# A convolution and a mixture of experts on one core: the outputs of the large tiles transposed by VectorE, stored in pieces, loaded back and gated on ACT

## The chip, the cores and the metric

The kernel runs on one core of one Trainium2 chip. Engines are named as in the profile: PE (TensorE), PEld (its weight loads), DVE (VectorE), ACT (ScalarE), POOL (GpSimd), SP (SyncE, which here only issues transfers). The metric is the device time of one execution in microseconds (us), median of several runs; smaller is better.

## The reference

```python
Xf = np.fft.rfft(x, n=2 * S, axis=1)            # x: 8 x 5696 x 128
y = np.fft.irfft(Xf * np.fft.rfft(h, n=2 * S, axis=0)[None], n=2 * S, axis=1)[:, :S]
x = y.reshape(B * S, D)                         # 45568 tokens of 128
logits = x @ w_gate + modality_bias[modality_id]
e_idx = np.argmax(logits, axis=1)
gate_w = softmax(logits)[np.arange(N), e_idx]
out[mask] = gate_w[mask, None] * (np.maximum(x[mask] @ w1[e], 0.0) @ w2[e])   # mask: tokens of expert e
```

A long convolution by Fourier transforms is followed by a layer of 8 experts (128 to 1024 to 128 features), where each token goes to one expert and its result is scaled by one gate value.

## The kernel before, in words

The program has two parts that overlap. The first (`stage1`, `stage23`, `stage4`) computes the convolution as two rounds of matrix products. Its last transform, `stage4`, makes token rows, finds each row's expert, position and gate value, and `dispatch` scatters the rows with indirect transfers from POOL into the DRAM array `rows`, where the tokens of one expert lie together. A row has 130 numbers: 128 features, the gate value, and the token's index in the output.

The second part (`Moe`) takes `rows` in tiles of consecutive tokens of one expert: 81 large tiles of 512 tokens (0 to 80 here) and then small ones of 256 tokens (81 to 100, and three more under a condition at run time). Tiles 0 to 35 belong to the first two levels, which are begun while `stage4` still produces rows; their outputs are held back (`NHELD`), stored to the DRAM array `late`, loaded again by `bring` into `ob`, and scattered later, between the outputs of later tiles.

A large tile t is worked in 8 steps (t, f), f = 0 to 7, a small one in 4. In a step PE runs `gemm1` (three products of 512 columns into a PSUM buffer `ph`: high and low parts of the float32 factors) and then `gemm2` of the step two earlier (three products into `po`, which gathers over all steps of a tile). From `ph`, ACT makes `hh` (relu, L647) and DVE makes `hl` (the low part, L648). So six products make a step, and `gemm2` of (t, 0) comes behind `gemm1` of (t, 2). `ph` has two PSUM buffers, and `po` has two. Once a tile, `prep` makes the operands of the next one: DVE transposes 32x32 blocks (`mxt`, L626; the 128-byte pieces in which the rows were loaded finish the transposition), ACT copies the high part (`mxh`, L629), DVE makes the low part (`mxl`, L630).

When a tile's `po` is done, ACT copies it to `ot` (L669), PE transposes it in four 128x128 pieces (`pxt`, L677), DVE multiplies by the gate value (`of`, L680), and POOL scatters 128 rows at a time to `out` (L709). For held tiles POOL also copies the indices into `held` (L683).

Order: within an engine, instructions run in program order. The SP queue is written out by hand: for each tile the weights of tile t+2 (2 MB, L613, taken only where the expert changes), the rows of tile t+3 (four transfers of 64 KB, L603, and one of gate values and indices, L605), then stores and loads of `late`. The order of ACT, DVE and POOL is set by a scheduler when the kernel is built; PE's too while `stage4` runs, and by hand behind it (tile 32 on in the program). `evenly` paces the scatters, a little under one a step, behind that step's ACT instruction.

Of the kernel before, what the change touches and what calls it, by code (L numbers as in the profile page):

```python
# [60 lines left out]
NLAST = 3  # L61
NHELD = LEVELS[0] + LEVELS[1]
SMALL = LEVELS[3] - NLAST
EVEN = ((NHELD + LEVELS[2]) * NSUB + SMALL * TSL // 128) / (8 * (LEVELS[2] - 2) + 4 * (SMALL - 3))
JOBS = [(lv, j) for lv, n in enumerate(LEVELS) for j in range(n)]
# [26 lines left out]
def conv_moe(  # L92
# [485 lines left out]
    class Moe:  # L578
        def __init__(self, wp, sp0, sp, pst, psh, pso):
            self.sp0, self.sp, self.pst, self.psh, self.pso = sp0, sp, pst, psh, pso  # L580
            self.slots = [wp[i].tile([128, 2, 2, FF], F32R, name=f"slot{i}") for i in range(NSLOT)]
            self.st = {}
# [3 lines left out]
            self.back, self.backs, self.credit = 0, [], 0.0  # L586

# [3 lines left out]
        def load(self, t):  # L591
            lv, j = JOBS[t]
            tab, src = self.tabs[lv]
            ts = TSL if lv == len(LEVELS) - 1 else TS
            ns = ts // 128
            r0 = nc.sync.value_load(tab[0:1, j:j + 1], min_val=0, max_val=E * REGION)
            rt = self.sp0.tile([128, TS], F32, name="mrt", bufs=4)
            mt = self.sp0.tile([128, NSUB, 2], F32, name="mmt", bufs=5)
# [6 lines left out]
            nc.sync.dma_start(mt[:, :ns], src[bass.ds(r0, ts), D:].rearrange("(c p) w -> p c w", p=128))  # L605
            self.st[t] = {"rt": rt, "mt": mt, "ts": ts, "ns": ns}
# [26 lines left out]
        def gemm1(self, t, f):  # L633
# [17 lines left out]
        def gemm2(self, t, f):  # L651
# [15 lines left out]
            if k == 7:  # L667
                ot = self.sp.tile([128, TS], F32, name="ot")
                nc.scalar.copy(ot[:, :ts], po)  # L669
                st["ot"] = ot  # L670

        def finish(self, t):
            st = self.st.pop(t)
            ns = st["ns"]
            pq = self.pst.tile([128, NSUB, 128], F32, name="pxt")
            for c in range(ns):
                nc.tensor.transpose(pq[:, c, :], st["ot"][:, c * 128:(c + 1) * 128], ident)  # L677
            of = self.sp.tile([128, NSUB, D], F32, name="of")
            rt = st["mt"]
            nc.vector.tensor_tensor(of[:, :ns], pq[:, :ns], rt[:, :ns, 0:1].to_broadcast([128, ns, D]), op=ALU.mult)  # L680
            ri = rt.bitcast(I32)
            if t < NHELD:
                nc.gpsimd.tensor_copy(self.held[:, t, :].unsqueeze(2), ri[:, :, 1:])  # L683
                nc.sync.dma_start(late_d[t], of.rearrange("p c d -> p (c d)"))
                return
            for c in range(ns):
                self.outs.append((t, c, ri[:, c, 1:2], of))

        def bring(self):
            if self.back < NHELD and len(self.backs) <= NSUB // 2:  # L690
                t = self.back
                self.back += 1
                of = self.sp.tile([128, NSUB, D], F32, name="ob")
                nc.sync.dma_start(of.rearrange("p c d -> p (c d)"), late_d[t])
                for c in range(NSUB):
                    self.backs.append((t, c, self.held[:, t, c:c + 1], of))

# [26 lines left out]
        def tiles(self, first, total):  # L724
# [11 lines left out]
            for g in range(len(steps) + LAG):  # L736
# [5 lines left out]
                if t < total:  # L742
                    self.gemm1(t, f)
                    dispatch(1, self.st[t]["act"])
                    self.evenly(self.st[t]["act"])
                    if t > NHELD:
                        self.bring()
                else:
                    self.scatter(1)
# [13 lines left out]
            if f < LAG:  # L763
                self.finish(total - 1)
            while self.outs or self.backs or self.back < NHELD:
                self.scatter(len(self.outs))
                self.outs, self.backs = self.backs, []
                self.bring()

# [10 lines left out]
    with tc.tile_pool(name="p4l", bufs=1, space=PSUM) as ps4l:  # L780
# [19 lines left out]
        with tc.tile_pool(name="moe", bufs=2) as sp, tc.tile_pool(name="moew", bufs=1) as wp, \  # L800
# [119 lines left out]
```

## Time and profile before

| | before |
|---|---|
| median of 3 runs | 2048.96 us (2048.7 to 2052.32) |
| the profiled execution | 2071.95 us; its span 2070.1 us |
| PE busy | 1976.8 us (95%) |
| DVE, ACT, POOL busy | 1448.5, 1129.2, 1115.2 us |
| mean granted TensorE clock | 0.984 |

Times in the views are counted from the start of the profiled span. A row of the timeline has start, duration, engine, line, operation and tiles, and in brackets the idle time before it with what ended it. A matmul's duration is longer than the distance to the next one's start, since they are pipelined. The profiled execution took 1% longer than the median run.

### The profile page before, as it was taken

To read this page: it belongs to the slowest core of one execution; us is meant where nothing else is said; L and a number is where in the kernel's file an instruction comes from. 1 tells how busy PE (TensorE), PEld (TensorE's weight loads), DVE (VectorE), ACT (ScalarE), POOL (GpSimd) and SP (SyncE) were. 2 spreads that over 40 slices of the span, in tenths; PEclk is the share of its full clock that TensorE was granted. 3 is DMA by queue.
4 is the path that set the end of the run, shared out by engine and by line. 5 is a ranking of instruction groups with operands and counts; after the bars stand their busy time and mean duration, and the time that the engine had idled before them with its cause. 6 is when DMAs were issued, how large, how long until landed. Compare 5 with 4: busy or idle time off the path is not lost. (4 is left out here: it accounts for less than half of the span.)

```text
span 2070.1 us, 32691 instructions
## 1 busy us (share of the span) xinstructions
PE 1976.8 (95%) x9114; PEld 1414.6 (68%) x9114; DVE 1448.5 (70%) x2478; ACT 1129.2 (55%) x2000; POOL 1115.2 (54%) x1085
## 2 busy tenths in 40 slices
PE   6889999999999997999999999999999999999996
PEld 5755555534444434878878778777787778778996
DVE  6659888886877996687677676756666666565553
ACT  5757777544444444666666566444544455454443
POOL 2127777673787783544344544614555555555544
PEclk9999999999999998999999999999999999999998
DMA  9999999989999997544465643353333343335443
GB/s 330 391 359 302 324 324 329 290 248 319 330 326 309 315 323 247 169 127 130 112 170 172 173 126 75 86 174 80 74 79 76 73 119 72 83 70 150 141 146 122
DMA packets 395831, 407.09 MB, mean 197 GB/s; under 512 B 242583, under 2 KB 277368, under 8 KB 393344
## 3 DMA queue, kind: packets, MB, share of 16 engines
q1 hardware_dynamic: 324496, 271.97, 44.3%
q10 hardware_dynamic: 47920, 85.94, 13.0%
q0 software_dynamic: 23232, 47.08, 6.6%
q8 instruction: 74, 1.21, 0.3%
q14 instruction: 109, 0.89, 0.1%
HBM read 396.70 MB, written 182.99 MB: 280 GB/s over the span
## 5 line engine op out<-in xcount | busy, mean ns | idle before, releaser
L648 DVE SCALAR_TENSOR_TENSOR hl<-ph,hh 128x512 fp32r<-128x512 f32 x728 | 496.1, 686 | 337.8 <-ACT hh L647 243.8
L647 ACT ACTIVATE hh<-ph 128x512 fp32r<-128x512 f32 x728 | 431.8, 598 | 469.2 <-PE ph L644 324.2
L320 POOL DMA_INDIRECT rows<-rt,idx x360 | 369.6, 1027 | 280.4 <-ACT hh L647 174.6
L290 POOL TENSOR_TENSOR t<-t,t 96x512 f32<-96x512 f32 x224 | 330.2, 1495 | 137.7 <-DVE t L283 120.1
L283 DVE TENSOR_TENSOR t<-px,hs 96x512 f32<-96x512 f32 x512 | 318.1, 677 | 63.1 <-PE px L280 27.2
L709 POOL DMA_INDIRECT out<-of,mmt x220 | 217.2, 987 | 222.2 <-ACT hh L647 172.6
L642 PE MATMUL ph<-mxh,slot 128*128 128x512 f32 (+1 forms) x808 | 319.9, 396 | 14.1 <-DVE hl L648 10.5
L664 PE MATMUL po<-hh,slot 128*128 128x512 f32 (+1 forms) x808 | 304.7, 377 | 8.3 <-ACT hh L647 8.2
L666 PE MATMUL po<-hl,slot 128*128 128x512 f32 (+1 forms) x808 | 300.7, 372 | 0.2 <-DVE hl L648 0.2
L644 PE MATMUL ph<-mxl,slot 128*128 128x512 f32 (+1 forms) x808 | 300.0, 371 | 0.0
L665 PE MATMUL po<-hh,slot 128*128 128x512 f32 (+1 forms) x808 | 299.6, 371 | 0.0
L643 PE MATMUL ph<-mxh,slot 128*128 128x512 f32 (+1 forms) x808 | 299.4, 371 | 0.0
L280 PE MATMUL px<-z,m 96*96 96x512 f32 x512 | 257.2, 604 | 4.0 <-DVE t L283 3.2
L263 ACT COPY ut<-pu 90x512 f32<-90x512 f32 x256 | 148.0, 581 | 127.5 <-PE pu L258 60.7
L709 POOL DMA_INDIRECT out<-ob,held x144 | 139.9, 971 | 121.5 <-ACT hh L647 81.8
L258 PE MATMUL pu<-t,mi 96*96 96x512 f32 x384 | 197.5, 606 | 4.7 <-ACT ut L263 2.1
L642 PEld LDWEIGHTS ph<-mxh,slot 128*128 128x128 f32 x808 | 152.6, 189 | 58.0 <-DVE hl L648 27.5
L664 PEld LDWEIGHTS po<-hh,slot 128*128 128x128 f32 x808 | 152.5, 189 | 38.2 <-ACT hh L647 12.1
L666 PEld LDWEIGHTS po<-hl,slot 128*128 128x128 f32 x808 | 152.4, 189 | 28.2 <-DVE hl L648 0.6
L644 PEld LDWEIGHTS ph<-mxl,slot 128*128 128x128 f32 x808 | 152.2, 188 | 28.0
L665 PEld LDWEIGHTS po<-hh,slot 128*128 128x128 f32 x808 | 152.6, 189 | 25.3
L643 PEld LDWEIGHTS ph<-mxh,slot 128*128 128x128 f32 x808 | 153.3, 190 | 18.0
(165 smaller groups left out, 2796.9 us busy)
## 6 DMA issues: line engine op xcount, KB each, us to landing
slot<-w12s SPq DMA_DIRECT2D x101, 2048.0 KB
z<-z SPq DMA_DIRECT2D x128, 360.0 KB
z<-z SPq DMA_DIRECT2D x45, 640.0 KB
z<-z SPq DMA_DIRECT2D x45, 512.0 KB
mrt<-rows SPq DMA_DIRECT2D x312, 64.0 KB
w12s<-ws ACTq DMA_DIRECT2D x32, 512.0 KB
u<-ua ACTq DMA_DIRECT2D x63, 256.0 KB
u<-ub ACTq DMA_DIRECT2D x63, 256.0 KB
```

The costliest lines, as they stand in the source:

```text
L283: prods[0] = nc.vector.tensor_tensor(prod[i, j].rearrange("p (b d) -> p b d", d=D), px[:KP].rearrange("p (b d) -> p b d", d=D), hs[:, j, k ...
L290: add = eng.tensor_tensor(y[:, i], y[:, i], prod[1, 1 - i], op=ALU.add if i else ALU.subtract)
L320: d = nc.gpsimd.indirect_dma_start(views[count[0] % NVIEW], bass.IndirectOffsetOnAxis(ap=idx[:, t:t + 1], axis=0), rt[:, t, :], None, boun ...
L642: nc.tensor.matmul(po, w[:, 0, 0, fs], st["xh"], start=True, stop=False)
L643: nc.tensor.matmul(po, w[:, 0, 1, fs], st["xh"], start=False, stop=False)
L644: nc.tensor.matmul(po, w[:, 0, 0, fs], st["xl"], start=False, stop=True)
L647: st["act"] = nc.scalar.activation(hh, ph, AF.Relu)
L648: nc.vector.scalar_tensor_tensor(hl, ph, 0.0, hh.bitcast(F32), op0=ALU.max, op1=ALU.subtract)
L664: nc.tensor.matmul(po, w[:, 1, 0, fs], hh[:, cs], start=k == 0, stop=False)
L665: nc.tensor.matmul(po, w[:, 1, 1, fs], hh[:, cs], start=False, stop=False)
L666: nc.tensor.matmul(po, w[:, 1, 0, fs], hl[:, cs], start=False, stop=k == 7)
L709: d = nc.gpsimd.indirect_dma_start(oviews[(t * NSUB + c) % NVIEW], bass.IndirectOffsetOnAxis(ap=ix, axis=0), of[:, c, :], None, bounds_che ...
```

## The change

The 81 large tiles take another way behind `gemm2`. DVE transposes `po` by 32x32 blocks straight into `ot` (one buffer instead of two). SP stores `ot` to `late` in four transfers of 64 KB, whose 128-byte pieces put the blocks in their places, so that `late` holds whole token rows. All large tiles, not only the first 36, are loaded back into `ob` (three buffers); six steps behind the load's place in the program ACT multiplies each 128 rows by their gate values in place (`gate`), and POOL scatters them. Gate values and indices stay in `near` and `held` from the first load on. ACT's copy, PE's four transposes, DVE's multiplication and POOL's copy of indices are gone for these tiles; the small tiles keep them. Second, once `stage4` is done (`alone`), every other `gemm1` writes into the two buffers `py` that `stage4` had used, so there are four for the first products.

```diff
-            self.held = wp[0].tile([128, NHELD, NSUB], I32, name="held")
+            near = wp[0].tile([128, NEAR, NSUB, 2], F32, name="near")
+            held = sp.tile([128, NBIG - NEAR, NSUB, 2], F32, name="held", bufs=1)
...
-            ph = self.psh.tile([128, TS], F32, name="ph")
+            ph = ps4.tile([128, TS], F32, name="py") if self.alone and f % 2 else self.psh.tile([128, TS], F32, name="ph")
...
-                ot = self.sp.tile([128, TS], F32, name="ot")
-                nc.scalar.copy(ot[:, :ts], po)
+                ot = st["ot"] = self.sp.tile([128, TS], F32, name="ot", bufs=1)[:, :ts]
+                if t < NBIG:
+                    nc.vector.transpose(ot, po)
+                else:
+                    nc.scalar.copy(ot, po)
...
+            if t < NBIG:
+                for j in range(0, D, BK):
+                    nc.sync.dma_start(late_d[t].rearrange("(n p) d -> p n d", p=BK)[:, :, j:j + BK],
+                                      st["ot"][j:j + BK].rearrange("p (n w) -> p n w", w=BK))
+                return
...
+        def bring(self, t):
+            if self.back < min(NBIG, t - 1) and len(self.ripe) * NSUB + len(self.backs) < (NOB - 1) * NSUB:
+                ob = self.sp.tile([128, NSUB, D], F32, name="ob", bufs=NOB)
+                nc.sync.dma_start(ob.rearrange("p c d -> p (c d)"), late_d[self.back].rearrange("(p c) d -> p (c d)", c=NSUB))
...
+                for c in range(NSUB):
+                    m = nc.scalar.activation(ob[:, c], ob[:, c], AF.Copy, scale=mt[:, c, 0:1])
...
+            moe.alone = True
```

DVE's order in the changed kernel, about tile 64 (numbers tell the buffers of one name apart; `po_17968` belongs to a tile t, `hl_18224` and `hl_18242` are the low parts of steps (t+2, 0) and (t+2, 1)):

```order
L655 SCALAR_TENSOR_TENSOR hl_18208<-py_18203,hh_18207 128x512 [waits Activation_49]
L655 SCALAR_TENSOR_TENSOR hl_18224<-ph_18219,hh_18223 128x512 [waits Activation_49]
L633 STREAM_TRANSPOSE mxt_18333<-mrt_17954 128x512 [waits DMAHW5_49,DMAHW6_49,DMAHW4_49,DMAHW3_49]
L655 SCALAR_TENSOR_TENSOR hl_18242<-py_18237,hh_18241 128x512 [waits Activation_49]
L637 TENSOR_TENSOR mxl_18336<-mxt_18333,mxh_18335 128x512 [waits Activation_49]
L677 STREAM_TRANSPOSE ot_18083<-po_17968 128x512 [waits DMAHW2_49,DMAHW3_49,DMAHW1_49,DMAHW0_49]
L655 SCALAR_TENSOR_TENSOR hl_18292<-ph_18287,hh_18291 128x512 [waits Activation_49]
```

The transposition of tile t's outputs stands behind the low part of (t+2, 1) and the `mxl` of the tile after, and waits for the four stores out of the one `ot`. From tile 42 to 77 three places alternate, twelve tiles each: this one, behind (t+2, 1) without an `mxl` between, and behind (t+2, 0). For the tiles up to 31 it stands behind (t+1, 0) or (t+1, 1).

PE's order in the changed kernel at the same tile (`po_18298` is tile t+2's, and so takes the PSUM buffer of `po_17968`):

```order
L671 MATMUL po_18132<-hh_18207,slot1_7160 128x512 [waits Activation_49]
L672 MATMUL po_18132<-hh_18207,slot1_7160 128x512
L673 MATMUL po_18132<-hl_18208,slot1_7160 128x512 [waits DVE_49]
L649 MATMUL ph_18287<-mxh_18174,slot2_7161 128x512
L650 MATMUL ph_18287<-mxh_18174,slot2_7161 128x512
L651 MATMUL ph_18287<-mxl_18175,slot2_7161 128x512
L671 MATMUL po_18298<-hh_18223,slot2_7161 128x512 [waits DVE_49,Activation_49]
```

Between the end of `gemm1` of (t+2, 1) and the first product into `po_18298`, PE has these six products; that first product now waits for DVE, and `gemm1` no longer does. Before, at such a place:

```order
L642 MATMUL ph_20703<-mxh_20595,slot1_7160 128x512 [waits DVE_49]
L643 MATMUL ph_20703<-mxh_20595,slot1_7160 128x512
L644 MATMUL ph_20703<-mxl_20596,slot1_7160 128x512
L664 MATMUL po_20716<-hh_20645,slot1_7160 128x512 [waits Activation_49]
L665 MATMUL po_20716<-hh_20645,slot1_7160 128x512
L666 MATMUL po_20716<-hl_20646,slot1_7160 128x512
L677 MATMUL pxt_20720<-ident_67,ot_20666 128x128 [waits Activation_49]
L677 MATMUL pxt_20720<-ident_67,ot_20666 128x128 x3
```

The four transposes went, and the wait moved from `gemm1` to `gemm2`.

SP's order in the changed kernel where the large tiles end (`ot_23377` is tile 80's; slot 2 takes the weights of tile 83):

```order
L620 DMA slot2_7161<-w12s 128x4096 [waits DMAHW2_49,PE_49]
...
L606 DMA mrt_23407<-rows 128x2x128 [waits DMAHW3_49]
...
L612 DMA mmt_23408<-rows 128x2x2 [waits DMAHW4_49]
L686 DMA late<-ot_23377 32x16x32 [waits DMAHW5_49,DVE_49]
L686 DMA late<-ot_23377 32x16x32 [waits DMAHW6_49]
L686 DMA late<-ot_23377 32x16x32 [waits DMAHW7_49]
L686 DMA late<-ot_23377 32x16x32 [waits DMAHW0_49]
```

The four stores of tile 80 stand in the queue behind the weights of tile 83 (register instructions between them are left out). And ACT's order at that place, where `ot_23502` is tile 81's copy into the one `ot` buffer:

```order
L713 ACTIVATE ob_23344<-ob_23344,held_7163 128x128 x3
L679 COPY ot_23502<-po_23422 128x256 [waits DMAHW5_49,DMAHW4_49,DMAHW6_49,DMAHW2_49,DMAHW7_49,DMAHW0_49,DVE_49]
L654 ACTIVATE hh_23573<-py_23566 128x512 [waits PE_49]
L654 ACTIVATE hh_23593<-ph_23586 128x512 [waits PE_49]
L636 CAST mxh_23606<-pxt_23603 128x256 [waits PE_49]
```

The copy, which waited only for PE before, now waits for the stores of tile 80, and the `hh` of the next steps stand behind it.

## Rows read from the trace of the kernel before

**Rows 1.** Windows: busy PE, PEld, DVE, ACT, POOL (instructions), granted clock, DMA share, GB/s.

```profile
850.00:900.00 50.00, 50.00 (x278) 39.84 (x276) 35.95 (x63) 33.78 (x60) 24.58 (x30) 1.00 0.60 168
...
1400.00:1500.00 100.00, 99.13 (x445) 79.54 (x444) 62.06 (x95) 50.38 (x87) 52.57 (x54) 1.00 0.35 78
```

**Rows 2.** Timeline of PE about the transposes of one large tile.

```profile
1606.03 0.39 PE L666 MATMUL po<-hl,slot 128*128 128x512 f32 x1
1606.26 0.60 PE L677 MATMUL pxt<-ident,ot 128*128 128x128 f32 x4
1606.62 0.48 PE L642 MATMUL ph<-mxh,slot 128*128 128x512 f32 x1
1606.93 0.39 PE L643 MATMUL ph<-mxh,slot 128*128 128x512 f32 x1
```

**Rows 3.** Timeline of ACT: the copies that end tiles 36, 51, 52 and 79.

```profile
1405.82 0.59 ACT L669 COPY ot<-po 128x512 f32<-128x512 f32 x1
...
1581.73 0.59 ACT L669 COPY ot<-po 128x512 f32<-128x512 f32 x1
...
1593.13 0.59 ACT L669 COPY ot<-po 128x512 f32<-128x512 f32 x1
...
1909.71 0.59 ACT L669 COPY ot<-po 128x512 f32<-128x512 f32 x1
```

**Rows 4.** Waits of PE, 1400 to 1900 us: total, times, longest.

```profile
PE ph L642 <- DVE hl L648: 3.6, 12, 0.6
```

**Rows 5.** Waits of PE, 1900 to 2060 us.

```profile
PE ph L642 <- DVE hl L648: 5.1, 8, 1.1
```

**Rows 6.** Groups by line: busy time, mean ns of one, idle time before them.

```profile
L677 PE MATMUL pxt<-ident,ot 128*128 128x128 f32 x364 | 56.3, 272 | 1.8 <-ACT ot L669 1.0 <-issue 0.9
L648 DVE SCALAR_TENSOR_TENSOR hl<-ph,hh 128x512 fp32r<-128x512 f32 x728 | 496.1, 686 | 337.8 <-ACT hh L647 243.8 <-issue 80.7 <-ACT ot L669 9.7
L680 DVE TENSOR_TENSOR of<-pxt,mmt 128x512 f32<-128x512 f32 (+1 forms) x101 | 63.5, 629 | 14.1 <-PE ph L644 5.2 <-PE pxt L677 3.6 <-PE py L400 3.4
L626 DVE STREAM_TRANSPOSE mxt<-mrt 128x512 f32<-128x512 f32 x78 | 54.8, 702 | 4.2 <-DMA mrt<-rows 3.4 <-DVE hl L648 0.5 <-issue 0.2
L630 DVE TENSOR_TENSOR mxl<-mxt,mxh 128x512 fp32r<-128x512 f32 x78 | 54.0, 692 | 39.6 <-ACT mxh L629 30.4 <-PE ph L644 6.5 <-issue 2.5
L647 ACT ACTIVATE hh<-ph 128x512 fp32r<-128x512 f32 x728 | 431.8, 598 | 469.2 <-PE ph L644 324.2 <-issue 51.5 <-DVE hl L648 20.0
L669 ACT COPY ot<-po 128x512 f32<-128x512 f32 (+1 forms) x101 | 54.9, 544 | 10.5 <-PE po L666 2.8 <-PE ph L644 1.5
L629 ACT CAST mxh<-mxt 128x512 fp32r<-128x512 f32 x78 | 48.4, 620 | 41.4 <-PE ph L643 31.6 <-issue 7.1 <-DVE mxt L626 2.6
L451 ACT ACTIVATE ex<-lg 128x96 f32<-128x96 f32 x30 | 8.6, 287 | 15.1 <-DVE lg L436 10.7 <-DVE mx L435 3.4 <-issue 0.9
L344 ACT ACTIVATE gp<-gs,sgn 128x192 f32<-128x192 f32 x18 | 7.2, 451 | 2.3 <-DMA gs<-in_gq 2.3
```

**Rows 7.** Timeline of SP: the transfers issued at the end of one large tile.

```profile
1605.06 0.08 SPq L613 DMA_DIRECT2D slot<-w12s  x1
1606.20 1.65 SPq L603 DMA_DIRECT2D mrt<-rows  x4
```

**Rows 8.** Windows about those loads of rows, and about a weight load.

```profile
1606.00:1610.00 4.00, 4.00 (x21) 3.26 (x20) 2.36 (x4) 1.56 (x3) 1.38 (x3) 1.00 0.56 83
...
1926.00:1931.00 5.00, 5.00 (x44) 5.00 (x43) 3.34 (x6) 2.58 (x6) 2.54 (x3) 1.00 0.92 388
```

**Rows 9.** Timeline of SP where the large tiles end.

```profile
1923.99 0.35 SPq L613 DMA_DIRECT2D slot<-w12s  x1
```

**Rows 10.** Timeline of POOL: the last two scatters.

```profile
2058.43 0.97 POOL L709 DMA_INDIRECT out<-of,mmt  x1 [0.30 <-issue]
2059.71 0.97 POOL L709 DMA_INDIRECT out<-of,mmt  x1 [0.30 <-issue]
```

**Rows 11.** Chain that ended last: a weight load beside the last transform.

```profile
1100.90 11.02 DMA slot<-w12s
```

More of the change, by code (lines that the diff above doesn't have):

```diff
@@ L581, in __init__ @@
             self.slots = [wp[i].tile([128, 2, 2, FF], F32R, name=f"slot{i}") for i in range(NSLOT)]
-            self.st = {}
+            self.st, self.alone = {}, False
             self.outs = []
             self.tabs = {}
-            self.held = wp[0].tile([128, NHELD, NSUB], I32, name="held")
-            self.back, self.backs, self.credit = 0, [], 0.0
+            near = wp[0].tile([128, NEAR, NSUB, 2], F32, name="near")
+            held = sp.tile([128, NBIG - NEAR, NSUB, 2], F32, name="held", bufs=1)
+            self.meta = [near[:, t] if t < NEAR else held[:, t - NEAR] for t in range(NBIG)]
+            self.back, self.ripe, self.backs, self.credit = 0, [], [], 0.0
         def on_pe(self, t):
@@ L597, in load @@
             rt = self.sp0.tile([128, TS], F32, name="mrt", bufs=4)
-            mt = self.sp0.tile([128, NSUB, 2], F32, name="mmt", bufs=5)
+            mt = self.meta[t] if t < NBIG else self.sp0.tile([128, TSL // 128, 2], F32, name="mmt", bufs=5)
             if self.on_pe(t):
@@ L677, in finish, with gate @@
                 nc.tensor.transpose(pq[:, c, :], st["ot"][:, c * 128:(c + 1) * 128], ident)
-            of = self.sp.tile([128, NSUB, D], F32, name="of")
+            of = self.sp.tile([128, TSL // 128, D], F32, name="of")
             rt = st["mt"]
-            nc.vector.tensor_tensor(of[:, :ns], pq[:, :ns], rt[:, :ns, 0:1].to_broadcast([128, ns, D]), op=ALU.mult)
+            nc.vector.tensor_tensor(of, pq[:, :ns], rt[:, :ns, 0:1].to_broadcast([128, ns, D]), op=ALU.mult)
             ri = rt.bitcast(I32)
[L682 to L685, printed above, removed]
             for c in range(ns):
                 self.outs.append((t, c, ri[:, c, 1:2], of))
-        def bring(self):
-            if self.back < NHELD and len(self.backs) <= NSUB // 2:
-                t = self.back
-                self.back += 1
-                of = self.sp.tile([128, NSUB, D], F32, name="ob")
-                nc.sync.dma_start(of.rearrange("p c d -> p (c d)"), late_d[t])
+        def bring(self, t):
+            if self.back < min(NBIG, t - 1) and len(self.ripe) * NSUB + len(self.backs) < (NOB - 1) * NSUB:
+                ob = self.sp.tile([128, NSUB, D], F32, name="ob", bufs=NOB)
+                nc.sync.dma_start(ob.rearrange("p c d -> p (c d)"), late_d[self.back].rearrange("(p c) d -> p (c d)", c=NSUB))
+                self.ripe.append([AGE, self.back, ob])
+                self.back += 1
+        def gate(self, after=None):
+            for it in self.ripe:
+                it[0] -= 1
+            while self.ripe and (after is None or self.ripe[0][0] < 0):
+                _, t, ob = self.ripe.pop(0)
+                mt = self.meta[t]
                 for c in range(NSUB):
-                    self.backs.append((t, c, self.held[:, t, c:c + 1], of))
+                    m = nc.scalar.activation(ob[:, c], ob[:, c], AF.Copy, scale=mt[:, c, 0:1])
+                    if after is not None:
+                        tc.add_manual_dep(m.ins, after.ins.name, PACED, reason="order")
+                    self.backs.append((t, c, mt.bitcast(I32)[:, c, 1:2], ob))
         def evenly(self, after):
@@ L746, in tiles @@
                     if t > NHELD:
-                        self.bring()
+                        self.gate(self.st[t]["act"])
+                        self.bring(t)
                 else:
@@ L764, in tiles @@
                 self.finish(total - 1)
-            while self.outs or self.backs or self.back < NHELD:
+            while self.outs or self.backs or self.ripe or self.back < NBIG:
                 self.scatter(len(self.outs))
+                self.gate()
                 self.outs, self.backs = self.backs, []
-                self.bring()
+                self.bring(total)
     fx = ExitStack()
@@ L913 @@
     args.append(scratch("w12s", (E, 128, 2, 2, FF)))
-    args.append(scratch("late", (NHELD, 128, TS)))
+    args.append(scratch("late", (NBIG, TS, D)))
     args.append(nc.dram_tensor("out", (NTOK, D), F32, kind="ExternalOutput").ap())
```

10 lines of the change are left out of this document (7 added, 3 removed).

## The prediction

> **What bounds the kernel now.** I read the windows first. From 850 us, where the tiles begin beside the last transform, PE is busy all the time, and in the stage behind it 99% of it [rows 1]; ACT, DVE, POOL and the transfers have a third or more to spare. So I look only for time that PE gains or loses, and for POOL at the very end. Next, the pace of a large tile: from the copy that ends tile 36 to the one that ends tile 79 lie 503.89 us, 11.72 a tile over 43 tiles, and a tile in which PE waits for nothing takes 11.4 (tiles 51 to 52) [rows 3]. So waits are 0.3 us a tile at most; the list of waits has 3.6 us in the whole stretch [rows 4] (its busy time counts the modelled ends of products, so it shows less than the pace does). I take 0.26.
>
> **What is removed.** Four transposes a tile, 81 tiles. Their mean duration is 272 ns [rows 6], but durations overlap. Read by starts instead: from the last product before them to the second one after them (1606.03 to 1606.93) it is 0.90 us, and two ordinary distances of 0.23 would be 0.46 [rows 2]. So PE loses 0.44 to 0.46 us a tile to the four; I take 0.46, 37 us in all 81. The Trainium skill (TensorE: Matmul & The Clock Gate, Part 4: PE-mode transpose) gives about 275 ns for a transposition inside a kernel; 324 of them by that figure would be 89 us. The trace agrees with the figure as a duration and not as what PE loses, and the sum goes by the starts.
>
> DVE: a multiplication out of PSUM (0.63 mean, small tiles in it) becomes a transposition of 128x512; the nearest rows are the transposition from SBUF, 0.70, and `hl` out of PSUM, 0.69 [rows 6]. I take 0.70; between 0.63 and 0.8 nothing changes by itself. ACT: the copy of 0.59 [rows 3] goes, four `gate` instructions of 128x128 come. The trace has none; 128x96 takes 0.29, 128x192 with a scale in pieces 0.45 [rows 6]. At 0.3 a tile costs 1.2 us, at 0.45 1.8, so ACT gets 0.6 to 1.2 more in 11.7. ACT is busy half the time [rows 1] and PE needs `hh` only two steps later: no cost, unless two gates fall together, 2.4 us against about 1.6 of slack. POOL's copies of indices are free either way: POOL is half idle.
>
> **Where the gain goes: the place of the transposition.** `po` has two buffers, so the first `gemm2` of tile t+2 must wait until DVE has transposed tile t. Before, ACT's copy freed the buffer at once. Now the order of DVE puts the transposition late. In the place shown, behind the low part of (t+2, 1) and the `mxl`, it can be reached only by this chain, counted from the end of `gemm1` of (t+2, 1): `hh` 0.60, `mxh` 0.62, `mxl` 0.69, transposition 0.70 [rows 6], with hand-offs of some 0.05 each, 2.8 us. PE has six products in that time, 6 x 0.23 = 1.38, of which 0.17 lies before the counted end (a product lasts 0.39 and the next starts after 0.23 [rows 2]): it is ready after 1.2 and waits 1.6. Without the `mxl` between, the chain is `hh`, `hl`, transposition: 2.1, wait 0.9. Behind (t+2, 0) PE has a step more, and waits for nothing. Twelve tiles of each kind: 12 x 1.6 + 12 x 0.9 = 30 us.
>
> The four `ph` buffers take away waits at `gemm1` (0.26 a tile), as the order shows: the `hl` they needed is now asked for by `gemm2`, five products (1.15 us) later.
>
> **The sum.**
> - Tiles 0 to 28, beside the transform: 29 x 0.46 = 13 less. There the transposition stands a tile earlier, so `po` makes no wait. But a weight load there can take 11 us [rows 11], and the stores stand behind it in the queue, with one `ot` buffer for all; I give 3 back: -10 (from -13 to +5).
> - Tiles 29 to 43: 15 x (0.46 + 0.26) = 11, of which some waits there come from loads that stay: -8 (-11 to -5).
> - Tiles 44 to 80: 37 x 0.72 = 27 less, 30 more: +4 (0 to +8).
> - The end of the large tiles. The copy of tile 81's outputs on ACT waits for tile 80's stores. These wait for DVE and stand behind a weight load, issued at 1923.99 [rows 9], which fills the queue until 1931 [rows 8]; with some 3 us for the stores themselves they land 10 us after tile 80's `po`, where ACT wants to copy after 6, and every `hh` behind it is late. Of the 4 to 8 us PE hides 1.6 by its lag: +6 (+3 to +11).
> - Small tiles: 5.1 us of waits for `hl` [rows 5] of which the four buffers can save up to 4: -4 (-6 to 0).
> - The tail: scatters are paced, a little under one a step, and start six steps later than before; by the rule of `evenly` eight are left behind the last step where three were, and each takes 1.28 us of POOL [rows 10]: +6 (+3 to +6.4).
>
> Together -6. The profiled execution took 1% longer than the median (2071.95 against 2048.96), a part that I leave alone: 2048.96 - 6 = 2043 us, with a range of its own of 2033 to 2055 when the bounds don't all fall on one side.
>
> **The stores.** SP issues four more transfers a tile; four cost it 1.65 us [rows 7], and it has nothing to do in the second half of a tile. The pieces of 128 bytes are writes, which the trace doesn't show at this size. As loads, 256 KB of them with one scatter beside them took a DMA share of 0.56 in 4 us, 2.2 us of all engines [rows 8]. The next transposition comes a tile later, 11.8 us, less its own 0.7 and the issue of 1.65: 9.4 us for the stores to land. So they hide until they take about four times what the loads take. The Trainium skill (DMA: Bandwidth & Descriptors, Specifications) says that below 512 B a transfer is done as read-modify-write. If that made a write twice as dear as these loads, 4.5 us, the sum would not change; no row here shows such a write. I take the loads' price.
>
> **Rivals.**
> - *The transpositions don't hold PE* (DVE reaches them earlier than the chain says, or the waits stand where PE waits anyhow): then tiles 44 to 80 give 27 and not -4, 31 us more, 2012. For it: DVE is busy only 62% of that stage. Against it: program order and the chain's four rows. Chance 0.15.
> - *The pieces are dear, on the slower side*: if four stores take over 9.4 us, `ot` holds DVE, and each microsecond beyond it costs one in every large tile behind the transform, 50 of them. At 10.5 that is 55 us: 2098. The loads at a quarter of that speak against it. Chance 0.08.
> - *Weight loads beside the transform* (also slower): where a tile there follows in 11.7 us and its weights take 11, the stores come behind them and 3 us of loads, and DVE waits some 5 us, PE some 3. At 8 of 29 tiles that is 24 instead of the 3 in the sum: 2064. From about 15 us lost, the gain of that stage is gone. Chance 0.15.
> - *No change in effect*, gains and waits cancelling exactly, lies inside the likeliest case.
>
> **How the numbers follow.** The likeliest case, 2043, has 0.60, and 0.02 is left for mishaps on either side. 0.2% is about what the measurement can tell from no change, 4 us: 2044.9 to 2053.1. Of the likeliest case I put half below 2044.9, a third within, a sixth above. So faster 0.15 + 0.31 = 0.46, within 0.2% 0.20, slower 0.10 + 0.15 + 0.08 + 0.01 = 0.34. The range of 8 in 10 runs from the first rival to the third: 2010 to 2066.
>
> **What would show it.** In the profile after: no transposes of 512-token tiles, and the tile pace beside the transform shorter by 0.46. Behind tile 43 PE waits at the first product into `po` for DVE's transposition, 1.6, 0.9 and 0 us in turn, and the pace stays within 0.2 of 11.72. No wait for DVE at `gemm1`. ACT waits some 5 us for a store at the copy of tile 81. POOL ends some 10 us behind PE. A pace under 11.3 there would make me wrong upwards in gain, DVE waiting for stores at the transposition downwards.

## The result, and the profile after

The changed kernel takes 2070.89 us (median of 4 runs, 2066.8 to 2075.87) where the kernel before takes 2050.64 (4 runs): a ratio of 1.0084 on record, 95% interval 1.0063 to 1.0105. It is slower by 0.84%, about 17 us; the two medians by themselves lie 20 us apart. The prediction said 2043, faster, with a range up to 2066: wrong in sign, and 5 us outside its range. A second series gave 1.0079 (1.0057 to 1.0102).

First the groups by line of the changed kernel, those that answer to [rows 6]:

```profile
L713 ACT ACTIVATE ob<-ob,held 128x128 f32<-128x128 f32 x308 | 96.6, 390 | 0.8 <-DMA ob<-late 0.6
L677 DVE STREAM_TRANSPOSE ot<-po 128x512 f32<-128x512 f32 x81 | 57.5, 709 | 6.7 <-PE po L673 6.0 <-DMA late<-ot 0.2
L691 PE MATMUL pxt<-ident,ot 128*128 128x128 f32 x40 | 8.0, 282 | 11.4 <-ACT ot L679 11.4
```

The transposes of the 512-token tiles are gone (364 on PE before, 40 now, all of small tiles). VectorE's transposition takes 0.709 us and a gate 0.39: both as forecast (0.70, and 0.3 to 0.45). VectorE waited 0.2 us for stores in the whole run. So neither of these two prices is off; what matters is who waits for the transposition.

The waits of PE from 1473 to 1900 us, which is tiles 44 to 79 (answers to [rows 4]; total, times, longest):

```profile
PE po L671 <- ACT ob L713: 16.9, 12, 1.4
PE po L671 <- ACT hh L654: 9.5, 12, 0.8
```

Twelve waits of 1.4 and twelve of 0.8, all at the first product into `po`; `hl` at `gemm1` is gone from the list. The list names ACT. One of the first twelve in the timelines of PE, VectorE and ACT, tile 56:

```profile
1619.40 0.39 PE L651 MATMUL ph<-mxl,slot 128*128 128x512 f32 x1
1621.20 0.47 PE L671 MATMUL po<-hh,slot 128*128 128x512 f32 x1 [1.41 <-ACT ob L713]
```

```profile
1619.09 0.69 DVE L655 SCALAR_TENSOR_TENSOR hl<-py,hh 128x512 fp32r<-128x512 f32 x1
1619.73 0.69 DVE L637 TENSOR_TENSOR mxl<-mxt,mxh 128x512 fp32r<-128x512 f32 x1
1620.34 0.71 DVE L677 STREAM_TRANSPOSE ot<-po 128x512 f32<-128x512 f32 x1
```

```profile
1620.38 1.27 ACT L713 ACTIVATE ob<-ob,held 128x128 f32<-128x128 f32 x4
```

VectorE goes through `hl`, `mxl` and the transposition, which ends at 1621.05; 0.15 us later PE starts. The product could have come 0.23 after the one at 1619.40, so it lost 1.57 us; the forecast for this place was 1.6. The gates of ACT, which the list names, touch none of the tiles of this product, and they run on to 1621.65, past its start. One of the other twelve, tile 55, lost 0.95 us (forecast 0.9):

```profile
1607.46 0.39 PE L651 MATMUL ph<-mxl,slot 128*128 128x512 f32 x1
1608.64 0.47 PE L671 MATMUL po<-hh,slot 128*128 128x512 f32 x1 [0.79 <-ACT hh L654]
```

In all 24 the trace has the transposition ending 0.15 us before the product starts, and the `hh` that the product reads, all that it needs of ACT, ending 2.9 to 3.5 us before. The third experiment moves the transposition. The pace follows in turn, read from the first product of tiles 55 to 58 (12.03, 12.59 and 11.19 us):

```profile
1604.19 0.40 PE L649 MATMUL ph<-mxh,slot 128*128 128x512 f32 x1
1616.22 0.39 PE L649 MATMUL ph<-mxh,slot 128*128 128x512 f32 x1
1628.81 0.39 PE L649 MATMUL ph<-mxh,slot 128*128 128x512 f32 x1
1640.00 0.40 PE L649 MATMUL ph<-mxh,slot 128*128 128x512 f32 x1
```

Where the large tiles end (answers to [rows 9]), timelines of SP, then ACT, then PE:

```profile
1924.34 0.34 SPq L620 DMA_DIRECT2D slot<-w12s  x1
...
1926.89 6.02 SPq L686 DMA_DIRECT2D late<-ot  x4
```

```profile
1934.95 0.37 ACT L679 COPY ot<-po 128x256 f32<-128x256 f32 x1 [8.41 <-DMA late<-ot]
```

```profile
1935.38 0.69 PE L691 MATMUL pxt<-ident,ot 128*128 128x128 f32 x2 [10.87 <-ACT ot L679]
```

The four stores of tile 80 take SP 6 us behind the weights, ACT's copy of tile 81 waits 8.4 for them, and PE 10.9. Behind that wait PE ran at the lower of its two clock levels (1.2 GHz), as two windows show (columns as in [rows 1]; the granted clock is 0.50): its products of 256 columns come 0.21 apart, where 0.12 lay between them before the wait.

```profile
1935.00:1937.00 2.00, 1.62 (x8) 1.62 (x9) 0.42 (x1) 0.33 (x1) 0.00 (x0) 0.50 0.13 46
1937.00:1940.00 3.00, 3.00 (x16) 3.00 (x16) 0.69 (x1) 0.65 (x2) 0.98 (x1) 0.50 0.29 66
```

The one profiled execution of the kernel before (2071.95 us) was not like the runs behind its median, and in three later series that kernel takes 2066 to 2088 in every run, so a ratio from such a series is marked "late starts" below, for what ACT does in most of their traces, and is compared with no other.

The parts of the span, from the first product of one tile to that of the next named, in us:

| | before, first profile | before, again | changed | 4 `ph` alone | changed, 2 `ph` | all in program order | best (scatter in every step) |
|---|---|---|---|---|---|---|---|
| tile 0 starts at | 808.5 | 811.4 | 813.9 | 810.8 | 809.2 | 810.4 | 812.2 |
| tiles 0 to 28 | 494.1 | 492.8 | 487.1 | 494.4 | 486.3 | 483.5 | 487.9 |
| 29 to 43 | 181.8 | 177.6 | 172.1 | 173.4 | 179.6 | 171.8 | 170.2 |
| 44 to 80 | 434.0 | 426.6 | 440.9 | 424.5 | 422.1 | 415.9 | 415.9 |
| 81 and 82 | 14.7 | 12.5 | 24.5 | 12.5 | 19.2 | 20.6 | 12.7 |
| 83 to 99 | 115.3 | 110.2 | 109.3 | 109.7 | 109.6 | 107.2 | 105.3 |
| tile 100 to the end | 21.7 | 23.4 | 26.2 | 22.5 | 26.7 | 28.9 | 21.0 |
| span | 2070.1 | 2054.5 | 2074.0 | 2047.8 | 2052.6 | 2038.3 | 2025.1 |

### The profile page after: what moved, and what is told of

The parts are those of the page before. It is cut to its first block, busy times and chain, and to the rows that moved or that the text cites. A ratio compares the mean times of both kernels' runs of the same rounds, so it can differ in the third digit from the quotient of the medians.

```text
span 2074.0 us, 32866 instructions
## 1 busy us (share of the span) xinstructions
PE 1948.7 (94%) x8790; PEld 1393.8 (67%) x8790; DVE 1450.5 (70%) x2478; ACT 1181.9 (57%) x2243; POOL 1112.6 (54%) x1049
## 5 line engine op out<-in xcount | busy, mean ns | idle before, releaser
L654 ACT ACTIVATE hh<-ph 128x512 fp32r<-128x512 f32 x496 | 295.7, 598 | 268.7 <-PE ph L651 248.7
L655 DVE SCALAR_TENSOR_TENSOR hl<-ph,hh 128x512 fp32r<-128x512 f32 x496 | 338.6, 685 | 156.8 <-ACT hh L654 144.5
L729 POOL DMA_INDIRECT out<-ob,held x308 | 306.7, 996 | 228.5 <-ACT ob L713 138.3
L655 DVE SCALAR_TENSOR_TENSOR hl<-py,hh 128x512 fp32r<-128x512 f32 x232 | 160.1, 690 | 153.4 <-ACT hh L654 152.5
L654 ACT ACTIVATE hh<-py 128x512 fp32r<-128x512 f32 x232 | 138.2, 596 | 139.9 <-PE py L651 122.4
L649 PE MATMUL ph<-mxh,slot 128*128 128x512 f32 (+1 forms) x536 | 208.3, 389 | 5.0 <-DVE sums L549 2.1
L650 PE MATMUL ph<-mxh,slot 128*128 128x512 f32 (+1 forms) x536 | 202.8, 378 | 0.0
L651 PE MATMUL ph<-mxl,slot 128*128 128x512 f32 (+1 forms) x536 | 202.0, 377 | 0.0
L284 PEld LDWEIGHTS px<-z,m 96*96 96x96 f32 x512 | 83.5, 167 | 120.1 <-issue 78.3
L262 PEld LDWEIGHTS pu<-t,mi 96*96 96x96 f32 x384 | 60.1, 168 | 90.6 <-issue 64.9
```

The source lines that it names most:

```text
L262: nc.tensor.matmul(pu[:KP], mi32[:, i, :], yl[:, i], start=True, stop=True)
L284: nc.tensor.matmul(px[:KP], mm, zbuf[k % NZ][:, i], start=True, stop=True)
L649: nc.tensor.matmul(po, w[:, 0, 0, fs], st["xh"], start=True, stop=False)
L654: st["act"] = nc.scalar.activation(hh, ph, AF.Relu)
L655: nc.vector.scalar_tensor_tensor(hl, ph, 0.0, hh.bitcast(F32), op0=ALU.max, op1=ALU.subtract)
L729: d = nc.gpsimd.indirect_dma_start(oviews[(t * NSUB + c) % NVIEW], bass.IndirectOffsetOnAxis(ap=ix, axis=0), of[:, c, :], None, bounds_che ...
```

## The experiments

**The kernel before, profiled again.** No edit.

> The kernel before, unchanged, profiled once more, because its profiled execution took 2071.95 us against a median of 2050.64 while the changed kernel's executions agree with its profile within some 9 us. Theory: the 20 us are lost in the stage ahead of the large tiles or beside the last transform, and a profile of an ordinary execution shows about 2049 us with the same pace behind the transform (615.8 us from the start of tile 29 to that of tile 81, within 2). Rival: the profiled execution was slow behind the transform, where the waits I meant to save don't exist otherwise; then those 615.8 us become some 600.

0.9997 (0.9977 to 1.0016), span 2054.5: the rival. From tile 29 to tile 81 it takes 604.2 us and not 615.8, and the waits of PE from 1450 to 1900 us are one:

```profile
PE ph L642 <- DVE hl L648: 0.6, 1, 0.6
```

[rows 4] has twelve such waits in about that stretch. What made them can be seen in the first profile, in tile 44. Its timeline of PE and of ACT:

```profile
1490.86 0.39 PE L644 MATMUL ph<-mxl,slot 128*128 128x512 f32 x1
...
1493.62 0.50 PE L642 MATMUL ph<-mxh,slot 128*128 128x512 f32 x1 [0.33 <-DVE hl L648]
```

```profile
1490.00 0.60 ACT L647 ACTIVATE hh<-ph 128x512 fp32r<-128x512 f32 x1 [1.32 <-DVE of L680]
1492.24 1.08 ACT L647 ACTIVATE hh<-ph 128x512 fp32r<-128x512 f32 x2 [1.64 <-PE ph L644]
```

and ACT at the same place of the second one:

```profile
1487.30 0.60 ACT L647 ACTIVATE hh<-ph 128x512 fp32r<-128x512 f32 x1 [1.23 <-PE ph L644]
1488.67 0.60 ACT L647 ACTIVATE hh<-ph 128x512 fp32r<-128x512 f32 x1 [0.77 <-PE ph L644]
```

The product ended at 1491.25; ACT, idle, started 1 us later and then ran two `hh` one right behind the other, and PE waited for the `hl` behind them. In the second profile, in which every engine runs the same instructions in the same order, the next `hh` comes in step. This execution, not the kernel, made the waits.

**Four buffers alone.** The kernel before, with

```diff
-            ph = self.psh.tile([128, TS], F32, name="ph")
+            ph = ps4.tile([128, TS], F32, name="py") if self.alone and f % 2 else self.psh.tile([128, TS], F32, name="ph")
...
+            moe.alone = True
```

> The kernel before with nothing of the change but the four PSUM buffers for the first products behind the last transform. Theory: the waits at the first product go, about 0.26 us in each of 52 large tiles and 4 to 6 us in the small ones: 13.5 + 5 = 18 less, about 2032 (2028 to 2040). Rival: the products run into the next wait (the copy of po on ACT, or hl asked for by the second product) and the time stays within 4 us of 2050.

0.9945 (0.9926 to 0.9965): 11 us, less than the 18 expected, and 6.7 between the two profiles. In tiles 44 to 80 they bring 2.1 us, since there is next to nothing to save; 4.2 come from tiles 29 to 43.

**VectorE in the order of the program.** The changed kernel, with

```diff
-            with tc.manual_schedule(engines={mybir.EngineType.PE}):
+            with tc.manual_schedule(engines={mybir.EngineType.PE, mybir.EngineType.DVE}):
```

> The changed kernel with VectorE behind the last transform in the order of the program, which puts the transposition of tile t straight behind hl of step (t+1, 1). Theory: PE waits at the first product into po for the transposition alone; with it early the pace is 11.05 to 11.2 us in all of tiles 44 to 80 instead of 11.92, 37 x 0.8 = 30 less, about 2040 (2036 to 2046). Rival: PE waits there for the gates on ACT, which the list of waits names for 16.9 of the 26.4 us; then the pace stays at about 11.9 and the time within 6 us of 2071.

0.9932 (0.9905 to 0.9959): 1.5% under the changed kernel, as expected. Tiles 44 to 80 take 410.9 us, 11.1 a tile, and PE's list of waits from 1473 to 1900 us is this alone:

```profile
PE po L673 <- DVE hl L655: 1.2, 2, 0.7
```

The gates are still there and no wait at the first product into `po` is; the transposition now ends some 10 us before that product. The scheduler gave ACT another order here too, so the run by itself doesn't tell VectorE's order from ACT's. The 24 waits above do: PE started 0.15 us behind the transposition each time, with its `hh` done for 2.9 us or more. So the wait hung on the place of the transposition. Tile 34 lost 8 us, seen on VectorE, then PE:

```profile
1365.77 0.72 DVE L677 STREAM_TRANSPOSE ot<-po 128x512 f32<-128x512 f32 x1 [8.16 <-DMA late<-ot]
```

```profile
1367.11 0.80 PE L673 MATMUL po<-hl,slot 128*128 128x512 f32 x1 [6.32 <-DVE hl L655]
```

The stores of the tile before stood on SP behind eight transfers of padding rows, and with strict order every `hl` stood behind the transposition. The wait itself is 6.3 us; behind it PE's products lay 0.43 apart instead of 0.23, at a granted clock of 0.50 from 1367 to 1370 us (1.2 GHz).

**A buffer of their own for the small outputs.**

```diff
-                ot = st["ot"] = self.sp.tile([128, TS], F32, name="ot", bufs=1)[:, :ts]
+                pool, name = (self.sp, "ot") if t < NBIG else (self.sp0, "mxt")
+                ot = st["ot"] = pool.tile([128, TS], F32, name=name, bufs=1)[:, :ts]
```

> The changed kernel with the outputs of the small tiles in a buffer of their own (that of mxt, idle by then) instead of the one that the stores of tile 80 still read. Theory: ACT's copy of tile 81 no longer waits for those stores, and PE's wait of 10.9 us in tile 82 goes, all but about 1: 10 less, about 2061 (2058 to 2064). Rival: the weights of the next tiles, queued behind the same stores on SP, are then what PE waits for, and less than half comes back: 2066 or more.

1.0061 (1.0042 to 1.0080): the rival. ACT's wait is gone, tiles 81 and 82 take 18.9 us instead of 24.5, and the rest is another wait of PE (1870 to 2070 us), for weights that SP issued late (timeline of SP):

```profile
PE ph L649 <- DMA slot<-w12s: 8.6, 3, 6.5
```

```profile
1911.02 3.94 SPq L703 DMA_DIRECT2D ob<-late  x2
1916.54 0.34 SPq L620 DMA_DIRECT2D slot<-w12s  x1
```

Two loads of `ob`, which wait for scatters to free a buffer (3.1 us by SP's list of waits), hold SP in front of them, and so do the stores of tile 79 before these, which wait 1.8 us for VectorE's transposition.

**The changed kernel with two `ph` buffers**: without the line `moe.alone = True`.

> The changed kernel without the four PSUM buffers for the first products. Times beside a kernel before of 2054 us, where the changed one stands at 2071. Theory: the buffers bring little, since in an undisturbed profile of the kernel before PE waits for hl only 0.6 us in 450: 0 to 0.15 us in each of 49 tiles, 2071 to 2079. Rival: behind the transposition's wait two buffers run dry once more, since hl of step (t+2, 1) is late together with the transposition: 0.7 us in two of three tiles, 25 more, about 2096.

0.998 (0.9957 to 1.0003; late starts, though its own profile has a single one): neither case, faster than either said. In its order of VectorE, which is the scheduler's, the transposition of tile t stands behind `hl` of (t+1, 4) or (t+1, 5) in all of tiles 41 to 78; with four buffers it is (t+2, 0) or (t+2, 1).

**Long stores.** The changed kernel; `late_d[t]` is written as it lies in `ot`.

```diff
-                    nc.sync.dma_start(late_d[t].rearrange("(n p) d -> p n d", p=BK)[:, :, j:j + BK],
-                                      st["ot"][j:j + BK].rearrange("p (n w) -> p n w", w=BK))
+                    nc.sync.dma_start(late_d[t].rearrange("(p c) d -> p (c d)", c=NSUB)[j:j + BK], st["ot"][j:j + BK])
```

> The changed kernel with the four stores of a tile written in runs of 2048 bytes a partition instead of pieces of 128 bytes; this leaves out the part of the transposition that the stores do, so the rows of the output are mixed up. Theory: the pieces are hidden; tiles 44 to 80 stay at 440.8 us within 1, beside the transform nothing moves by more than 2, and only the wait of tile 82, which hangs on the stores behind a weight load, gets shorter by 2 to 4: 2067 (2064 to 2072). Rival: the pieces slow the loads beside the transform and the weights behind it: 8 us or more less, 2063 or under.

1.0188 (1.0139 to 1.0237; late starts). Inconclusive: with other stores the scheduler gave VectorE and ACT another order.

**Program order from the sixth tile on.** `next(tiles)` forty times under the old line, then the new one of the third run.

> As the run with VectorE in the order of the program, but from the sixth tile of the stage on, past the eight transfers of padding rows behind which that run's VectorE waited for the rows of a tile (tile 34 took 19.3 us there against 11.0). Theory: that wait goes and nothing takes its place, 8 less: 0.984 to 0.987 of the kernel before, 2036 beside 2054 (2031 to 2040; before 2054). Rival: strict order costs the same somewhere else, where VectorE stands at another late load: 2042 or more.

0.9942 (0.9913 to 0.9971; late starts), so not to be held against 0.9932. Tile 34's loss is gone (29 to 35 take 86.8 us instead of 90.1). What VectorE stood at there was the stores, and not the rows of a tile, as the expectation has it.

**Weights first.** The own buffer, and `self.bring(t)` put behind `load_weights` and `load` in a step.

> The changed kernel with the small outputs in a buffer of their own, and with the load of ob put behind the load of weights in a step. In the run with the own buffer alone PE waited 6.5 us for the weights of tile 82, issued on SP behind two loads of ob that waited for scatters. Theory: that wait goes and with it the rest of the loss there: tiles 81 and 82 take 12.5 to 14 us instead of 18.9 and 24.5, and the time is some 10 less than the changed kernel's, 2061 beside 2054 (2057 to 2065). Rival: the weights wait for the slot itself or for the transfers in front, and the time stays within 4 of the run with the own buffer alone, 2066 to 2073.

1.0384 (1.0341 to 1.0426; late starts); see its second run below.

**The changed kernel again.**

> The changed kernel once more, beside the kernel before on the same chip, because on one chip the kernel before took 2072 and on others 2050. Theory: on a chip where the kernel before takes about 2052, the ratio is that of the first comparison, 1.006 to 1.010, and tiles 44 to 80 take 440.8 us within 1, with 11.2, 12.05 and 12.55 us in turn. Where the kernel before takes about 2072, VectorE's late transposition adds to the pauses of ACT that such executions show, and the changed kernel is slower by more than 1.2%. Rival: the pauses fall into the waits for the transposition, and the ratio there is under 1.005.

1.0079 (1.0057 to 1.0102), the kernel before at 2055; tiles 44 to 80 take 440.9 us. What it would be with late starts wasn't seen.

**ACT and POOL in program order too**, from the sixth tile on:

```diff
+            with tc.manual_schedule(engines={mybir.EngineType.PE, mybir.EngineType.DVE, mybir.EngineType.Activation, mybir.EngineType.Pool}):
```

> The changed kernel with VectorE, ACT and POOL in the order of the program from the sixth tile of the stage behind the transform. Theory: ACT's order mattered for nothing, the pace in tiles 44 to 80 is 11.05 to 11.2 us, and the time is that of the run with VectorE alone without its lost 8 us: 0.984 to 0.988 of the kernel before. Rival: gates at a fixed place, four in a row with a load that lands late, hold up hh: over 0.995.

0.9943 (0.9924 to 0.9963): faster than the changed kernel by 1.4%, and the same as with VectorE alone within the intervals; the expected 0.984 to 0.988 missed. Tile 34's 8 us are back, but 5 are lost in tiles 44 to 80, where tiles 60 and 77 take 13.6 and 13.2 us, and 2 in the tail.

**Long stores on that base**, from tile 44 on, every engine in the same order.

> The same, with the stores of tiles 44 to 80 in runs of 2048 bytes instead of pieces of 128 bytes; the order of every engine is the same, and the rows of those tiles come out mixed up, since the stores leave out their part of the transposition. Theory: the pieces are hidden, tiles 44 to 80 take the same within 1.5 us, and only the wait at the first small tiles gets shorter: ratio to the run with pieces 0.996 to 1.000. Rival: 128-byte pieces slow the loads and the issue on SP: 0.15 us or more a tile, 6 us in all, 0.994 or less.

0.9929 (0.9907 to 0.9950), 0.9986 of the run with pieces. Windows from 1450 to 1900 us, first with pieces, then with long stores (columns as in [rows 1]):

```profile
1450.00:1900.00 450.00, 439.56 (x1932) 354.85 (x1932) 281.46 (x433) 280.48 (x619) 256.52 (x264) 1.00 0.64 142
```

```profile
1450.00:1900.00 450.00, 444.28 (x1953) 358.56 (x1951) 285.19 (x438) 283.06 (x623) 260.78 (x267) 1.00 0.57 143
```

The pieces cost 0.07 of the transfer engines' time, 31.5 us or 0.85 a tile over 37 tiles, and hide: tiles 44 to 80 take 415.9 us with them and 414.7 without, tiles 81 and 82 20.6 and 18.8.

**The repairs together**: program order, own buffer, and

```diff
-                        self.bring(t)
+                        if t >= NBIG or 1 < f < 7:
+                            self.bring(t)
```

> All engines in the order of the program, the small outputs in a buffer of their own, and the loads of ob of the large tiles issued only between the third and seventh step of a tile, so that no weight load stands behind one that waits for scatters. Theory: PE's wait at tile 82 (7 to 11 us in the runs so far) goes, and the rest is as with the order alone: 0.979 to 0.984 of the kernel before, about 2012 to 2021 beside 2054. Rival: the weights of tile 82 come as late as before, because the slot or the transfers in front hold them: 0.985 or more.

0.9898 (0.9872 to 0.9925). Tiles 81 and 82 take 12.55 us, as before the change; but the small tiles take 112.8 and the tail 33.3, so the ratio missed.

**Two `ph` buffers, second run.**

> The changed kernel with two PSUM buffers once more, since the run of it fell in a time in which the kernel before took 2072, and there it was at 0.998 of it. In its order of VectorE the transposition of tile t stands right behind hl of step (t+2, 0) or earlier with no mxl ahead of it, in nearly all tiles, where the changed kernel has it behind (t+2, 1) in two of three. Theory: so the four buffers are what made the transposition late, PE waits at po for 3 us or less in tiles 44 to 80, these take 416 to 422 us (440.8 with four buffers), and the time is 0.994 to 1.000 of the kernel before. Rival: without pauses PE reaches po sooner and waits there as with four buffers: 434 us or more, 1.004 or over.

0.9999 (0.9984 to 1.0013). PE's waits from 1473 to 1900 us:

```profile
PE ph L649 <- DVE hl L655: 5.9, 23, 0.3
```

No wait at `po`; tiles 44 to 80 take 422.1 us. So the change without its four buffers is worth nothing either way, the four buffers alone 0.55% less, and both together 0.84% more.

**Own buffer and placed loads**, VectorE's order left to the scheduler.

> The changed kernel with the small outputs in their own buffer and with the loads of ob of large tiles only between the third and seventh step, its order of VectorE otherwise left to the scheduler. Theory: tiles 81 and 82 take 12.5 to 14 us (24.5 in the changed kernel, 18.9 with the own buffer alone), tiles 44 to 80 stay at 440 us within 4, and the time is 8 to 12 less than the changed kernel's: 1.002 to 1.004 of the kernel before. Rival: what is gained there comes back in the small tiles or the tail, as with the own buffer alone: 1.006 or more.

1.0006 (0.9988 to 1.0023), faster than expected and not for the reason given: the moved loads also changed VectorE's order, for most tiles to (t+1, 7), (t+2, 0), (t+2, 1) in turn, so that one tile in three is long instead of two (tiles 44 to 80: 424.3 us). Tiles 81 and 82 still take 17.5: PE waits 4.8 us for weights there, in front of which SP's stores wait 2.6 for VectorE's late transposition. So the placed loads alone don't repair this place; with program order beside them the two tiles took 12.55 us.

**A scatter in every step**: the repairs together, and `EVEN = 1.0`, where the formula gives 0.895.

> The run of all three repairs with one number more changed: a scatter may go out in every step (1.0) instead of in 0.895 of them, because that run left 33 us from the first product of the last small tile to the end where the kernel before has 23. Theory: the scatters that wait behind the last product go earlier, the tail takes 25 to 28 us, and the time is 0.984 to 0.987 of the kernel before. Rival: POOL is held by late loads of ob and not by the allowance, and the time stays within 0.2% of 0.990.

0.9871 (0.9851 to 0.9891), median 2026.0: the best version, 1.3% under the kernel before. Its last transposes on PE and last scatter on POOL (answers to [rows 10]), and below them the same two of the changed kernel:

```profile
2012.21 0.44 PE L692 MATMUL pxt<-ident,mxt 128*128 128x128 f32 x2 [0.52 <-ACT mxt L680]
...
2014.67 0.98 POOL L730 DMA_INDIRECT out<-of,mmt  x1 [0.30 <-DVEq L741]
```

```profile
2055.92 0.44 PE L691 MATMUL pxt<-ident,ot 128*128 128x128 f32 x2 [0.52 <-ACT ot L679]
...
2062.88 0.98 POOL L729 DMA_INDIRECT out<-ob,held  x1 [0.30 <-DMA out<-of,mmt]
```

POOL ends 3.0 us behind PE instead of 7.5.

**Three runs with late starts.** The weights first again, and the best version with two `ph` buffers, twice.

> The changed kernel with the small outputs in their own buffer and each load of ob behind the load of weights of its step, once more: the first run of it took 1.038 of the kernel before in a time in which that kernel itself took 2072. Its engines have the order of the run with the own buffer alone but for SP, where a load of ob stands in another place seven times. Theory: the 66 us came from that time, in which ACT starts late, and not from the seven moves; where the kernel before takes about 2052, this one is at 1.000 to 1.006 of it, with tiles 81 and 82 in 12.5 to 18 us. Rival: the moved loads land late and the gates hold ACT: 1.02 or more in any time.

> The best version so far (all engines in the order of the program, own buffer, loads of ob in the middle of a tile, a scatter in every step) with two PSUM buffers for the first products instead of four. Theory: with the order fixed the four buffers bring what they bring to the kernel before, 0.3 to 0.8%: this one is at 0.990 to 0.995 of the kernel before where the best is at 0.987. Rival: with the transposition early there are no waits at the first product, and both are the same within 0.2%.

> The best version with two PSUM buffers instead of four, once more, since its first run (1.025) fell in a time in which the kernel before took 2078. Theory: where the kernel before takes about 2052, the four buffers bring 0.3 to 0.8% with the order fixed, and this one is at 0.990 to 0.995 of it. Rival: both are the same within 0.2%, 0.985 to 0.989. Should the kernel before take over 2065 again, the run says nothing on this.

1.0423 (1.0397 to 1.0450), 1.0250 (1.0220 to 1.0280) and 1.0238 (1.0194 to 1.0282), with the kernel before at 2078, 2078 and 2081. All three were to be read beside a kernel before of 2052, so what they were to tell stays open: whether the moved loads cost anything of themselves, and whether the four buffers bring anything once the order is fixed. From 1480 to 1900 us their traces have 36 `hh` that start late by 65.0 us in all, 37 by 38.8 and 48 by 40.8, counted as in the last section (15 by 13.2 in the first profile of the kernel before). How much of that is the version and how much the time stays open too.

## Why the prediction was wrong, by its own steps

| term | predicted | against the first profile | against the second |
|---|---|---|---|
| tiles 0 to 28 | -10 (-13 to +5) | -7.0 | -5.7 |
| 29 to 43 | -8 (-11 to -5) | -9.7 | -5.5 |
| 44 to 80 | +4 (0 to +8) | +6.8 | +14.2 |
| 81 and 82 | +6 (+3 to +11) | +9.8 | +12.0 |
| small tiles | -4 (-6 to 0) | -6.0 | -0.9 |
| tail | +6 (+3 to +6.4) | +4.6 | +2.9 |
| sum | -6 | -1.5 | +17.0 |

(Tile 0 starts between 804 and 817 us in all these runs; that isn't counted.)

- **The step that failed** is the first: "So waits are 0.3 us a tile at most ... I take 0.26", together with the 1% by which the profile stood above the median, "a part that I leave alone". Those waits, and the 5.1 us of [rows 5], were of that execution: the second profile has one wait of 0.6 in the one stretch and none for `hl` in the other. Without them a large tile takes 11.53 us (426.6 / 37) and not 11.72, and the four buffers, priced at 0.26 a tile, save 0.06 (2.1 us in 37 tiles, in the run with them alone). The 11.4 taken for a tile without a wait is also the shortest of three in turn (11.4, 11.5 and 11.6 us in the second profile). Between the two profiles lie 7.4 us in tiles 44 to 80, 4.2 in 29 to 43, 2.2 in 81 and 82, and 5.1 in the small tiles: 19 of the 23 us between -6 and +17. The rest is the sizes below.
- **Transposes removed**: 0.46 us a tile. Tiles 37 to 43, without a wait in either, went from between 11.4 and 11.6 us (second profile) to between 10.9 and 11.2, 0.44 a tile; right. Beside the transform only 0.2 a tile shows; where the other half went wasn't found.
- **The place of the transposition**: right in place, chain, turn and size (1.57 and 0.95 us lost where 1.6 and 0.9 were forecast; pace 11.92 against a forecast of 11.84). Moving it took the waits away. What the prediction didn't see is its link with the other half: with two buffers the scheduler puts the transposition a chain earlier.
- **The end of the large tiles**: right mechanism, mis-sized. The stores landed 12.5 us after tile 80's transposition began (1922.4), not 10; ACT wanted its copy after 4.1, not 6, so it waited 8.4, and PE hid nothing. The transposition itself began 5.3 us after tile 80's last product (1917.1): the late place, priced for tiles 44 to 80, had no part in this term. Nor had the lower clock behind the wait: the two tiles cost 12.0 us more where PE waited 10.9. A second wait, for weights that SP issued late, lay under it.
- **The tail**: right in kind, over-sized: +2.9 against the second profile where +6 was forecast, with 7.5 us from PE's end to POOL's and not 10; the second profile of the kernel before has 3.0 (2042.08 to 2045.06).
- **The stores** hide, as said. The Trainium skill (DMA: Bandwidth & Descriptors, Specifications), which the prediction weighed, has transfers under 512 B done as read-modify-write, below line rate. The 0.85 us a tile agree with its direction, and the time didn't follow.
- **The rivals**: none came. Transpositions that don't hold PE are what VectorE's program order gave, 410.9 us in tiles 44 to 80; VectorE waited 0.2 us for stores in the whole run, so neither the pieces nor a weight load beside the transform held it.

## What to carry to other kernels

When the profiled execution stands a per cent above the median of the runs, take a second profile before any small wait in it is priced: here waits of 0.6 us, behind an engine that started late with nothing pending, belonged to the execution. When a copy that frees a PSUM buffer moves to an engine whose order a scheduler sets, read its new place in the order, for every version: a second edit that only adds buffers can move it, and two edits that are harmless or good alone can cost together. And where a list of waits names an engine, look for the instructions that the waiting one's own tiles need, and for the last of these to end: here the list named ACT in all 24 cases, for instructions that just happened to end then, and it was VectorE.

## What the runs showed of the hardware

In the first profile of the kernel before, and in most traces of the series marked so, ACT starts late while SP issues transfers in pieces. Counted in the trace over every `hh` whose last product ends between 1480 and 1900 us, late is a start more than 0.3 us after the later of that end and the end of ACT's instruction before. In the first profile of the kernel before 15 of 286 are late, 13.2 us in all, and 14 of the 15 while SP issues the loads of rows, 13 of them with the small load behind these; in the second profile none of 291, in the changed kernel's none of 282. In the best version with two buffers, first run, it is 37 of 247, 38.8 us in all, and PE's waits for `hl` from 1473 to 1900 us become:

```profile
PE ph L649 <- DVE hl L655: 50.9, 56, 1.2
```

SP stands still in the same executions, which tells them apart more sharply: of its own register instructions (MOVE and FUSED_REGOPS) between 1480 and 1900 us, 50 of 526 take over 0.25 us in the first profile of the kernel before and 20 to 51 in each of the seven profiles of the marked series, the changed kernel with two buffers among them (20). In the second profile of the kernel before, in both of the changed kernel's and in every other unmarked one, none does.

The same chip showed it in one series and not in another (the kernel before at 2072 and 2055), so it isn't a property of one chip. What brings it on wasn't found.
